# Constants and residual reloads issued by GpSimd, decay loads placed after a batch's three corrections, and a step budget of 1700 in place of 3500

## Chip, cores and metric

The kernel runs on one core of one Trainium2 chip. The metric is the device time of one execution in microseconds (us). Of the kernel before there are three runs: 947.62, 949.55 and 951.24 us, with a median of 949.55 us. The profiled execution, from which all rows below come, took 947.54 us; its span, from the first to the last recorded instruction, is 945.4 us.

## What is computed

Four batches of 768 steps go through three stages. The first is a linear recurrence with complex decays, for 8 heads of 48 channels:

```python
mag = sqrt(a_re**2 + a_im**2); scale = minimum(mag, 0.999) / (mag + 1e-6)
S_re, S_im = ar*S_re - ai*S_im + k v^T, ar*S_im + ai*S_re     # one step t
y[t] = q[t] @ S_re
```

The second is a mixer: with the token weights `u = x + (relu(x^T w_tok1) w_tok2)^T`, then with the channel weights `x2 = u + relu(u w_ch1) w_ch2` (384 to 1536 to 384). The third is a LayerNorm with gain `g_ln` and a second channel layer of the same size: `out = x2 + relu(LN(x2) w_ch1) w_ch2`.

## The kernel before

Rows are put on 128 partitions, three tiles of 128 channels for one batch. Every float32 product that must stay exact is split in two float16 parts, a high and a low one, and is three matmuls (`mm3`, lines 582 to 584).

Four Python generators write the program, and a driver at the end of `tile_kernel` interleaves them.

- `gen_E` does the **decay work** of one batch after the other on VectorE (DVE) and ScalarE (ACT). `gen_A` normalizes the decays and scans them over 16 steps (line 231 on ACT is its first operation; `cmul` is one scan step), `gen_L2` does the second level of the scan on small tiles, and `gen_C` forms the corrections of one tile of 128 channels: cumulated decays, their inverses, and q and k multiplied with them. `gen_C` ends with DMAs (lines 358 and 359) that put q and k into the heads' tiles `stk`. Almost all of its DVE instructions carry line 178, the line of the helper that records them. The decays of a batch lie in one buffer `aj`; `load_a(b, i)` (line 63, SyncE's queue SP) loads tile i of batch b into it, which can start when the corrections of that tile are done with the buffer.
- `gen_P` does the **heads**: 8 for each batch, in TensorE (PE) matmuls of 96 to 128 columns, with copies on ACT and DVE (lines 421 to 500). Their outputs `xh` and `xl` are the x of the mixer.
- `gen_W` splits the weights during the first batch.
- `gen_M` is the **mixing**: for each batch 48 steps, 12 for each half of the tokens and each of the two layers. In a step PE makes 9 matmuls of 384 columns into a bank, `relu_split` (lines 590 and 592) turns it into a high and a low half of `hid` on ACT and DVE, and PE makes 9 more with it. Behind a half's first layer comes `gen_LN`; three steps before the end of its second layer the residual is loaded back into `o` (line 784), which shares its one buffer with the LayerNorm's `xc`. Between two batches stand `tok1` and `tok2`, the token layers: `tok1` reads all eight heads.

What is done beside a mixing step is set by **budgets**. After each step the driver calls `run_E(budget)`, which pulls decay work until its own estimates (the numbers that `gen_E` yields: 470, 870, 1200 and so on) have used the budget up, or until the generator says "wait", which ends the call too. The budget is `EB` in the mixing of batches 2 to 4, `EB0` and `EB1` in that of batch 1, and `ET` in the token layers. All of it stands on line 1127. In the mixing of batch b the decay work is that of batch b+1, and, when that is done, of batch b+2, whose corrections must wait until heads have freed their tiles. The order on each engine follows from this program and from a list scheduler that may move neighbours past each other.

The constants `cst` (identity, mask and others, 129.5 KB) are loaded at line 78 behind the twelve first decay loads in SP's queue; the first operation that needs them is the ACT copy `eye_h` (line 98).

Of the kernel before, what the change touches and what calls it, by code (L numbers as in the profile page):

```python
# [17 lines left out]
B, H, S, D = 4, 8, 768, 48  # L18
# [18 lines left out]
def tile_kernel(ctx: ExitStack, tc: tile.TileContext, a_in, qk_in, v_in, aq2_in, v2_in, wt_in, wm1_in, wm2_in, w64_in, g_in, c_in, out):  # L37
    nc = tc.nc
    V, A, T, G = nc.vector, nc.scalar, nc.tensor, nc.gpsimd
    x2_d = tc.dram_tile([2 * B, 3, P, HB], F32, name="x2_d")  # L40
# [34 lines left out]
    eye_h = ap.tile([P, P], F16, name="eye_h")  # L75
    bias = cp.tile([P, 6], F32, name="bias")
    gl = cp.tile([P, 3], F32, name="gl")
    nc.sync.dma_start(out=cst, in_=c_in)
    wstat = cp.tile([P, 28], F32, name="wstat")
    rstat = cp.tile([P, 6 * B], F32, name="rstat")  # L80
    pstat = cp.tile([P, B, 3 * NCH], F32, name="pstat")
# [109 lines left out]
    def gen_E():  # L191
        V = Rec()
        nxt_q = [load_qk(0, j // 2, j % 2) for j in range(6)]
        load_w(1)
        for b in range(B):
            rec[0] = b == 0
            Ct = ap.tile([P, 3, 6 * 24], F32, tag="I", name="I")
            W = ap.tile([P, 2, 3, NCH], F32, tag="W", name="W")
            sq = ap.tile([P, 2, 3 * NCH], F32, tag="sq", name="sq")
            st = ap.tile([P, 2, 3 * NCH], F32, tag="st", name="st")  # L200
            V.memset(W[:, 0, :, 0:1], 1.0)
            V.memset(W[:, 1, :, 0:1], 0.0)
            for part in PARTS if b == 0 else ((0, 1, 2),):
                for x in gen_A(b, part):
                    yield x
                for x in gen_L2(b, part, Ct, W, sq, st):
                    yield x
                yield "C"
                for i in part:
                    for x in gen_C(b, i, Ct, st, nxt_q):  # L210
                        yield x
                    if b and b + 1 < B:
                        load_a(b + 1, i)
                    yield ("done", b, i)
                if b == 0 and part[-1] == 2:
                    for i in range(3):
                        load_a(1, i)

    av = aj.rearrange("p x (j k r) -> p x j k r", j=6, k=KB)

# [511 lines left out]
    def gen_M():  # L732
# [10 lines left out]
        for b in range(B):  # L743
            for _ in tok2(b, r1, (0, 1, 2) if b else (1, 2)):
                yield "tok"
            ln = iter(())
            if b == 0 and IL < FT:
                g = [mlp(wm1, 0, 0 < LNPE), mlp(wm1, 1, 1 < LNPE, ("sc", "tr", "y"))]
                for s in range(FT + 1 + IL):
                    for half in range(2):  # L750
                        if not 0 <= s - half * IL <= FT:
                            continue
                        k, acc = next(g[half])
                        if half:
                            next(ln, None)
                        if k < FT:
                            yield "step"
                        else:
                            for _ in ln:
                                pass  # L760
                            ln = gen_LN(half, acc)
                            next(ln)
            for half in range(0 if b or IL >= FT else 2, 2):
                for k, acc in mlp(wm1, half, 2 * b + half < LNPE):
                    next(ln, None)
                    if k < FT:
                        yield "step"
                for _ in ln:
                    pass
                ln = gen_LN(2 * b + half, acc)  # L770
                next(ln)
            for half in range(2):
                n = 2 * b + half
                for k, acc in mlp(wm2, half):
                    next(ln, None)
                    if half and b + 1 < B:
                        if k == 2:
                            tokw(b + 1, 0)
                        if k == K_TOK:
                            yield "x"  # L780
                            r1 = tok1(b + 1)
                    if k == FT - 3:
                        o = ap.tile([P, 3, HB], F32, tag="xc", name="o", bufs=1)
                        nc.sync.dma_start(out=o, in_=x2_d[n].rearrange("c p s -> p c s"))
                    if k < FT:
                        yield "step"
                for c in range(3):
                    t = tmp()
                    V.scalar_tensor_tensor(out=t, in0=acc[c][:, 0:HB], scalar=1 / (WS * WS), in1=rs[n], op0=ALU.mult, op1=ALU.mult)
                    V.scalar_tensor_tensor(out=o[:, c], in0=o[:, c], scalar=1 / US, in1=t, op0=ALU.mult, op1=ALU.add)  # L790
                    nc.sync.dma_start(out=out[c, :, n * HB:(n + 1) * HB], in_=o[:, c])
            yield ("done", b)
# [243 lines left out]
    for b in range(B):  # L1036
        k = 0
        while True:
# [21 lines left out]
            for _ in range(2):  # L1060
                n = st["p"]
# [42 lines left out]
NDW = 2  # L1104
CG, CGS = -1, 0
IL = 12
# [17 lines left out]
TGO, TGE, FILL, FK = ("m1", "sc", "m1", "m2"), ("sc", "m2", "m1", "m2"), 0, 0  # L1124
GC, WPE, SPE = 0, 0, 0
YH = 32
SR=1;GC=1;SPE=0;CD=2;LNPE=2;NKICK=0;NKT=1;K_TOK=12;YH=12;NDW=2;NHID=3;NST=3;NV=2;NSK=0;TGO=("m1","sc","m1","m2");PR=0.5;P0=-4;EB=3500;ET=2500;QH=16;WOFF=130;WSTEP=10;EB0=500;EB1=5000;KE=12;DH=1;IL=5;W0=4;NWARM=(0,0);NWB=(0,0);WG=4;WPE=0;EG=7;NWE=0;CGS=0;NS0=6;NSM=99;NSY=3
NV, TH, TP = 3, 4, 3
_INS = ["a", "qk", "v", "aq2", "v2", "wt", "wm1", "wm2", "w64", "g", "c"]

# [55 lines left out]
```

## Time and profile before

| | |
|---|---|
| runs (us) | 947.62, 949.55, 951.24; median 949.55 |
| profiled execution, span (us) | 947.54, 945.4 |
| PE busy | 826.7 us, 87% of the span |
| DVE busy | 736.4 us, 78% |
| ACT busy | 504.5 us, 53% |
| GpSimd (POOL) busy | 59.8 us, 6% |
| chain that ended last | PE 42%, DVE 32%, DMA 10%, issue 7%, ACT 6% |
| DMA | 108.28 MB, mean 115 GB/s |

The page's strip of 40 slices shows three regimes: PE idle and DVE full for the first three slices, both nearly full until about 650 us, and then PE full with DVE at two to six tenths. A busy PE is not yet a PE at its peak, as matmuls overlap; and an engine's idle time counts only where it is on the chain that ends last. The windows below cut the span at `hid` instructions, one stretch for each batch's mixing.

### The profile page before, as it was taken

Reading aid. Unit: us, or ns where it says so; the run is one execution under the profiler, and the core shown is the slowest. Engines: PE = TensorE matmul, PEld = TensorE weight load, DVE = VectorE, ACT = ScalarE, POOL = GpSimd, SP = SyncE. Lnnn points to the kernel's source line nnn. Section 1 sums busy time; section 2 is a strip of 40 time slices with the busy share of each in tenths; the row PEclk is TensorE's granted clock in tenths of the full one; section 3 lists DMA queues with packets and bytes.
Section 4 is the critical chain, followed back from the end, with each engine's and each line's share of the span. In section 5 each row is a group of like instructions: output and inputs, shape, how many; then the busy total and the mean of one; then the engine's idle time right before and its main releaser. Section 6 shows DMA issues by size and latency. Waiting matters only on the chain.

```text
span 945.4 us, 15969 instructions
## 1 busy us (share of the span) xinstructions
PE 826.7 (87%) x5786; PEld 561.7 (59%) x5786; DVE 736.4 (78%) x1588; ACT 504.5 (53%) x1383; POOL 59.8 (6%) x113
## 2 busy tenths in 40 slices
PE   0018998999899899998999998899999999999996
PEld 0007986556567677565666665566766666656563
DVE  6998889999997889987899999897766523264533
ACT  5123356643545586436689952773866524363542
POOL 0000101001030100001100000100000000011110
PEclk9999987999999999998999999899999999999998
DMA  8024576314476350214525010541200102356562
GB/s 291 0 55 119 190 247 209 119 51 169 140 234 179 90 155 14 93 40 127 136 56 148 20 58 33 160 104 60 57 33 26 52 1 92 132 165 215 189 228 95
DMA packets 45287, 108.28 MB, mean 115 GB/s; under 512 B 5904, under 2 KB 28560, under 8 KB 45200
## 3 DMA queue, kind: packets, MB, share of 16 engines
q1 hardware_dynamic: 36816, 61.57, 22.1%
q0 software_dynamic: 8384, 45.62, 14.6%
q8 instruction: 47, 0.77, 0.3%
q14 instruction: 40, 0.33, 0.1%
HBM read 77.20 MB, written 11.01 MB: 93 GB/s over the span
## 4 chain that ended last, share of the span: by engine, by line
PE 42%; DVE 32%; DMA 10%; issue 7%; ACT 6%; SPq 3%; POOL 0%; DVEq 0%; ACTq 0%; POOLq 0%
PE m L583 12%; PE m L582 11%; PE m L584 11%; DVE t L178 6%; DVE aj L178 5%; DVE p L178 4%; DVE hid L592 3%; DMA stk<-t 2%; DMA aj<-in_a 2%; DMA stk<-qk 2%; PE sc L441 2%; DVE pad L533 1%; DMA raw<-in_wm 1%; DVE qk L178 1%; DVE w L549 1%
## 5 line engine op out<-in xcount | busy, mean ns | idle before, releaser
L592 DVE SCALAR_TENSOR_TENSOR hid<-m,hid 128x384 f16<-128x384 f32 x198 | 109.1, 552 | 113.8 <-ACT hid L590 113.3
L582 PE MATMUL m<-u,w 128*128 128x384 f16 x576 | 188.9, 328 | 1.9 <-DVE u L642 1.2
L583 PE MATMUL m<-u,w 128*128 128x384 f16 x576 | 189.0, 328 | 1.3 <-DVE u L703 1.2
L584 PE MATMUL m<-u,w 128*128 128x384 f16 x576 | 188.9, 328 | 0.0
L590 ACT ACTIVATE hid<-m 128x384 f16<-128x384 f32 x198 | 96.0, 485 | 170.8 <-PE m L584 169.7
L583 PE MATMUL m<-hid,w 128*128 128x384 f16 x540 | 176.8, 328 | 8.6 <-DVE hid L592 8.5
L584 PE MATMUL m<-hid,w 128*128 128x384 f16 x540 | 176.7, 328 | 0.0
L584 PEld LDWEIGHTS <-w 128*128 128x128 f16 x1176 | 115.8, 98 | 88.5 <-issue 19.9
L583 PEld LDWEIGHTS <-w 128*128 128x128 f16 x1176 | 116.4, 99 | 73.8 <-issue 4.8
L582 PEld LDWEIGHTS <-w 128*128 128x128 f16 x1176 | 115.6, 99 | 74.0 <-issue 6.3
L582 PE MATMUL m<-hid,w 128*128 128x384 f16 x540 | 127.6, 326 | 1.6 <-ACT hid L590 1.3
L178 DVE SCALAR_TENSOR_TENSOR t<-t 128x384 f32<-128x384 f32 x120 | 64.3, 549 | 8.8 <-ACT t L231 5.7
L428 PE MATMUL m<-cst,stk 96*128 96x96 f32 x10 | 2.5, 377 | 71.1 <-DMA stk<-qk 71.1
L178 DVE TENSOR_TENSOR p<-aj 128x288 f32<-128x288 f32 (+2 forms) x150 | 52.4, 390 | 0.7
L178 DVE TENSOR_TENSOR t<-aj,I 128x768 f32<-128x768 f32 x40 | 36.3, 952 | 12.5 <-DMA stk<-t 9.4
L441 PE MATMUL sc<-stk 96*128 96x128 f32 x300 | 44.8, 284 | 1.2 <-DVE r L446 1.2
L428 PEld LDWEIGHTS m<-cst,stk 96*128 96x128 f32 x10 | 1.8, 231 | 71.4 <-issue 67.5
L441 PEld LDWEIGHTS sc<-stk 96*128 96x128 f32 x300 | 41.0, 197 | 4.1 <-DVE r L446 1.6
L516 POOL DMA_DIRECT2D raw<-in_wm x48 | 25.9, 540 | 213.4 <-DVE sq L561 85.2
L590 ACT ACTIVATION_READ_ACCUMULATOR hid<-m 128x1 f32 x198 | 38.5, 194 | 0.0
L562 ACT ACTIVATE sq<-sq 128x768 f16<-128x768 uint8 x28 | 23.6, 843 | 27.8 <-DVE sq L561 27.8
L536 ACT ACTIVATE w<-raw 128x768 f16<-128x768 f32 x28 | 25.3, 904 | 24.0 <-DVE raw L534 22.7
(273 smaller groups left out, 1692.6 us busy)
## 6 DMA issues: line engine op xcount, KB each, us to landing
raw<-in_wm POOLq DMA_DIRECT2D x48, 768.0 KB, 4.7
qk<-in_qk SPq DMA_DIRECT2D x23, 384.0 KB, 4.5
aj<-in_a SPq DMA_DIRECT2D x9, 768.0 KB, 6.5
stk<-t SPq DMA_DIRECT2D x40, 144.6 KB, 3.3
stk<-qk SPq DMA_DIRECT2D x40, 144.6 KB, 3.1
raw<-in_wt SPq DMA_DIRECT2D x6, 768.0 KB, 5.9
v<-in_v SPq DMA_DIRECT2D x32, 144.0 KB, 2.2
x_d<-xc SPq DMA_DIRECT2D x24, 192.0 KB, 2.2
```

Of the source, the lines that this page charges most:

```text
L178: r = getattr(nc.vector, n)(*a, **k)
L441: last = T.matmul(sc[:, (c % 3) * P:(c % 3 + 1) * P], qc(c, 1), qc(c, 0), start=True, stop=True)
L516: (nc.sync if n < NSY else nc.gpsimd).dma_start(out=raw.bitcast(U8), in_=w_src[n].bitcast(U8)[:, 3:3 + 8 * S])
L533: V.scalar_tensor_tensor(out=pad[0].bitcast(U8).rearrange("p (a b) -> p a b", b=4)[:, :, 3], in0=byte, scalar=3, in1=byte, op0=ALU.logical ...
L536: wact[n] = A.activation(out=dst[:, :, 0], in_=w, func=AF.Copy, scale=WS).ins
L549: wop[n] = V.scalar_tensor_tensor(out=dst[:, :, 1], in0=w, scalar=WS, in1=dst[:, :, 0], op0=ALU.mult, op1=ALU.subtract).ins
L562: A.activation(out=t[:, HB:2 * HB].bitcast(F16), in_=bad_, func=AF.Copy, accum_out=wstat[:, n:n + 1])
L582: T.matmul(out_, wh, xh_, start=first, stop=False)
L583: T.matmul(out_, wh, xl_, start=False, stop=False)
L584: T.matmul(out_, wl, xh_, start=False, stop=last)
L590: A.activation(out=hl[:, 0], in_=p, func=AF.Relu, accum_out=hstat[:, n_h[0]:n_h[0] + 1])
L592: last[:] = [V.scalar_tensor_tensor(out=hl[:, 1], in0=p, scalar=0.0, in1=hl[:, 0], op0=ALU.max, op1=ALU.subtract).ins]
```

## The change

Four edits are made. The constants are loaded from GpSimd's queue in place of SP's. The residual reload `o` goes to GpSimd's queue too. The three decay loads of the next batch are written after the corrections of all three tiles (they stood after each tile for batches 2 and 3; for batch 1 they stood there already). And `EB` is 1700 in place of 3500. In the new file lines above 210 keep their numbers, and those behind are two lower.

```diff
-    nc.sync.dma_start(out=cst, in_=c_in)
+    nc.gpsimd.dma_start(out=cst, in_=c_in)
...
                 for i in part:
                     for x in gen_C(b, i, Ct, st, nxt_q):
                         yield x
-                    if b and b + 1 < B:
+                    yield ("done", b, i)
+                if part[-1] == 2 and b + 1 < B:
+                    for i in range(3):
                         load_a(b + 1, i)
-                    yield ("done", b, i)
-                if b == 0 and part[-1] == 2:
-                    for i in range(3):
-                        load_a(1, i)
...
-                        nc.sync.dma_start(out=o, in_=x2_d[n].rearrange("c p s -> p c s"))
+                        nc.gpsimd.dma_start(out=o, in_=x2_d[n].rearrange("c p s -> p c s"))
...
-SR=1;GC=1;SPE=0;CD=2;LNPE=2;NKICK=0;NKT=1;K_TOK=12;YH=12;NDW=2;NHID=3;NST=3;NV=2;NSK=0;TGO=("m1","sc","m1","m2");PR=0.5;P0=-4;EB=3500;ET=2500;QH=16;WOFF=130;WSTEP=10;EB0=500;EB1=5000;KE=12;DH=1;IL=5;W0=4;NWARM=(0,0);NWB=(0,0);WG=4;WPE=0;EG=7;NWE=0;CGS=0;NS0=6;NSM=99;NSY=3
+SR=1;GC=1;SPE=0;CD=2;LNPE=2;NKICK=0;NKT=1;K_TOK=12;YH=12;NDW=2;NHID=3;NST=3;NV=2;NSK=0;TGO=("m1","sc","m1","m2");PR=0.5;P0=-4;EB=1700;ET=2500;QH=16;WOFF=130;WSTEP=10;EB0=500;EB1=5000;KE=12;DH=1;IL=5;W0=4;NWARM=(0,0);NWB=(0,0);WG=4;WPE=0;EG=7;NWE=0;CGS=0;NS0=6;NSM=99;NSY=3
```

(On the last line only `EB` differs.)

What this does to the order of instructions is shown at three places. First, ACT at the start of the program, before (`t` and `u` are the scratch tiles of the first two decay pieces):

```order
L231 ACTIVATE t<-aj 128x768
L235 ACTIVATE t<-t 128x384
L236 ACTIVATE t<-t,bias 128x384
L237 ACTIVATE t,rstat<-t 128x384
L231 ACTIVATE u<-aj 128x768
L235 ACTIVATE u<-u 128x384
L236 ACTIVATE u<-u,bias 128x384
L98 ACTIVATE eye_h<-cst 128x128
L733 ACTIVATE gstat<-gl 128x3
L541 ACTIVATE eye_w<-cst 128x128
L542 ACTIVATE eye_m<-cst 128x128
L237 ACTIVATE u,rstat<-u 128x384
```

and with the change:

```order
L229 ACTIVATE t<-aj 128x768
L98 ACTIVATE eye_h<-cst 128x128
L539 ACTIVATE eye_w<-cst 128x128
L540 ACTIVATE eye_m<-cst 128x128
L233 ACTIVATE t<-t 128x384
L234 ACTIVATE t<-t,bias 128x384
L235 ACTIVATE t,rstat<-t 128x384
L229 ACTIVATE u<-aj 128x768
L233 ACTIVATE u<-u 128x384
L234 ACTIVATE u<-u,bias 128x384
L731 ACTIVATE gstat<-gl 128x3
L235 ACTIVATE u,rstat<-u 128x384
```

The three copies of the constants moved from behind the second piece's exponent to directly behind the first piece's square; the small operation on the gain `gl` stayed ahead of the second piece's last ACT operation.

Second, DVE where the mixing of batch 2 ends and the token layer of batch 3 begins (the two `hid` rows at the end are those of `tok1`), before:

```order
L178 COPY I<-W 128x36
L178 TENSOR_TENSOR t<-aj,I 128x2x16x24 x4
L789 SCALAR_TENSOR_TENSOR r<-m_6790,rs 128x384
L789 SCALAR_TENSOR_TENSOR r<-m_6791,rs 128x384
L789 SCALAR_TENSOR_TENSOR r<-m_6792,rs 128x384
L178 TENSOR_TENSOR aj<-t 128x2x384 x2
L790 SCALAR_TENSOR_TENSOR o<-o,r 128x384 x2
L592 SCALAR_TENSOR_TENSOR hid<-m_7455,hid 128x384
L790 SCALAR_TENSOR_TENSOR o<-o,r 128x384
L592 SCALAR_TENSOR_TENSOR hid<-m_7456,hid 128x384
```

and with the change:

```order
L178 TENSOR_TENSOR p<-aj 128x288 x2
L178 TENSOR_TENSOR aj<-p 128x6x24 x2
L178 TENSOR_TENSOR p<-aj 128x288 x2
L787 SCALAR_TENSOR_TENSOR r<-m_6444,rs 128x384
L787 SCALAR_TENSOR_TENSOR r<-m_6445,rs 128x384
L787 SCALAR_TENSOR_TENSOR r<-m_6446,rs 128x384
L178 TENSOR_TENSOR aj<-p 128x6x24 x2
L788 SCALAR_TENSOR_TENSOR o<-o,r 128x384 x3
L178 TENSOR_TENSOR p<-aj 128x288 x2
L590 SCALAR_TENSOR_TENSOR hid<-m_7161,hid 128x384
L590 SCALAR_TENSOR_TENSOR hid<-m_7162,hid 128x384
```

Before, the decay work of batch 4 is here through its scan and its second level and in its first correction; with the change it is still in the scan (`p<-aj`, `aj<-p`). Counted over the whole order up to the first of these two `hid` rows, 58 DVE instructions of line 178 stand later with the change: 6 of `p<-aj`, 8 of `aj<-p`, 38 small ones of the second level, 4 of `t<-aj,I` and 2 of `aj<-t`. The program's last line-178 row stands ahead of the 12th `hid` row of the mixing of batch 3 before, and ahead of its 30th with the change. Of the mixings of batch 2 and of batch 3, five `hid` rows follow the last head's last DVE row (`xl`) before, and two with the change.

Third, GpSimd's queue in the second half of the mixing of batch 1 and at the start of the next (`t<-st` and `qk<-st` are the copies that a correction waits for before its DMAs), before:

```order
L516 DMA raw<-in_wm 128x6144
L599 DMA tokw<-tokw_d 128x3072 x2
L332 COPY t<-st 128x3
L332 COPY qk<-st 128x3
L332 COPY t<-st 128x3
L332 COPY qk<-st 128x3
L599 DMA tokw<-tokw_d 128x3072 x2
```

and with the change:

```order
L514 DMA raw<-in_wm 128x6144
L330 COPY t<-st 128x3
L330 COPY qk<-st 128x3
L597 DMA tokw<-tokw_d 128x3072 x2
L782 DMA o<-x_d 128x3x384
L330 COPY t<-st 128x3
L330 COPY qk<-st 128x3
L330 COPY t<-st 128x3
L330 COPY qk<-st 128x3
L782 DMA o<-x_d 128x3x384
L597 DMA tokw<-tokw_d 128x3072 x2
```

The two reloads of batch 1 stand on both sides of the copies of its third correction tile; in SP's queue they are gone.

## Rows read from the trace of the kernel before

**Rows 1.** Windows: length, then PE, PEld, DVE, ACT, POOL busy (instructions), PEclk, DMA.

```profile
179.40:383.90 204.50, 195.02 (x1346) 131.32 (x1345) 190.49 (x371) 111.72 (x291) 19.66 (x27) 1.00 0.41 128
383.90:589.30 205.40, 191.91 (x1460) 125.61 (x1460) 190.24 (x430) 130.81 (x380) 8.90 (x18) 0.98 0.27 76
589.30:651.90 62.60, 57.41 (x440) 38.60 (x440) 53.96 (x91) 40.58 (x111) 5.82 (x9) 0.95 0.45 121
651.90:783.50 131.60, 131.45 (x1022) 87.13 (x1020) 72.83 (x135) 72.39 (x226) 0.00 (x0) 1.00 0.13 39
783.50:934.60 151.10, 149.16 (x932) 90.39 (x933) 66.25 (x133) 71.08 (x200) 13.51 (x25) 1.00 0.51 167
```

**Rows 2.** Windows of line 178 alone, in the mixing of batch 2.

```profile
383.90:589.30 205.40, 107.37 (x255) 0.98 0.27 76
```

**Rows 3.** Waits of PE, 383.9 to 589.3 us: total, times, longest.

```profile
PE m L583 <- DVE hid L592: 6.2, 6, 2.2
PE m L582 <- DVE hid L592: 1.9, 1, 1.9
```

**Rows 4.** Waits of PE, 589.3 to 783.5 us.

```profile
PE m L582 <- DVE hid L592: 3.1, 1, 3.1
PE m L582 <- DVE u L642: 2.4, 4, 0.8
```

**Rows 5.** Timeline of PE around a wait: start, duration, instruction.

```profile
433.94 0.33 PE L584 MATMUL m<-u,w 128*128 128x384 f16 x1
...
439.34 0.52 PE L584 MATMUL m<-hid,w 128*128 128x384 f16 x1
439.66 0.52 PE L583 MATMUL m<-hid,w 128*128 128x384 f16 x1
```

**Rows 6.** Groups of DVE instructions by shape: busy us, mean ns, idle before.

```profile
L178 DVE TENSOR_TENSOR p<-aj 128x288 f32<-128x288 f32 x90 | 36.8, 449 | 0.3
L178 DVE TENSOR_TENSOR t<-aj,I 128x768 f32<-128x768 f32 x40 | 36.3, 952 | 12.5 <-DMA stk<-t 9.4 <-DMA stk<-qk 2.3 <-issue 0.7
L178 DVE TENSOR_TENSOR aj<-p 128x144 f32<-128x144 f32 x90 | 23.3, 299 | 0.3
L178 DVE TENSOR_TENSOR aj<-t 128x768 f32<-128x768 f32 x20 | 18.5, 949 | 0.6 <-DMA aj<-in_a 0.6
```

**Rows 7.** Line 178 by operation: duration in ns, min/median/max.

```profile
L178 DVE TENSOR_TENSOR I<-p x40: 176/243/291, 43.5 to 581.4; 128x126 f32<-128x126 f32 x12, 128x72 f32<-128x72 f32 x8, 128x108 f32<-128x108 f32 x6, 128x84 f32<-128x84 f32 x4
```

**Rows 8.** Timeline of ACT, first 13 us, with the idle time ahead.

```profile
5.75 0.52 ACT L235 ACTIVATE t<-t 128x384 f32<-128x384 f32 x1 [0.62 <-DVE t L178]
...
11.71 0.31 ACT L98 ACTIVATE eye_h<-cst 128x128 f16<-128x128 f32 x1 [1.28 <-DMA cst<-in_c]
11.92 0.19 ACT L733 ACTIVATE gstat<-gl 128x3 f32<-128x3 f32 x1
...
12.42 0.51 ACT L237 ACTIVATE u<-u 128x384 f32<-128x384 f32 x1
```

**Rows 9.** Timeline of DVE, the instruction that this delays.

```profile
13.05 1.15 DVE L178 SCALAR_TENSOR_TENSOR u<-u 128x384 f32<-128x384 f32 x2 [2.09 <-ACT u L237]
```

**Rows 10.** DMA issues: queue, count, KB each, median us to landing.

```profile
raw<-in_wm POOLq DMA_DIRECT2D x48, 768.0 KB, 4.7
...
aj<-in_a SPq DMA_DIRECT2D x9, 768.0 KB, 6.5
...
o<-x_d SPq DMA_DIRECT2D x8, 576.0 KB, 4.1
...
cst<-in_c SPq DMA_DIRECT2D x1, 129.5 KB, 4.4
gl<-in_g SPq DMA_DIRECT2D x1, 1.5 KB, 4.0
```

**Rows 11.** Waits of SP's queue at the residual reload.

```profile
SPq L784 <- DVE u L703: 17.2, 3, 8.4
```

**Rows 12.** Timelines of PE and DVE: a late head's first transposes, its last DVE instruction.

```profile
744.68 0.58 PE L428 MATMUL tr<-cst,stk 96*128 96x96 f32 x5
...
761.89 0.46 DVE L397 SCALAR_TENSOR_TENSOR xl<-y,xh 128x288 f16<-128x288 f32 x1 [1.56 <-ACT xh L396]
```

## Prediction, made before the changed kernel ran

> **What bounds the kernel now.** I read the page's strip first, then windows cut at `hid` rows, then PE's waits in each window, then single rows. The windows [rows 1] have one line for each batch's mixing, and batch 3's is cut in two. In the last two lines PE is busy for 131.45 of 131.60 and 149.16 of 151.10 us: there PE is the bound, and DVE has 72.83 and 66.25 us of work. In the mixing of batch 2 PE is idle for 205.40 - 191.91 = 13.5 us, and in the first 62.6 us of batch 3's for 5.2 us. DVE is busy there for 190.24 us of 205.40 and 53.96 of 62.60. So for these 268 us DVE is about as long as PE, and behind them it is half empty. That is the imbalance on which the change acts.
>
> That PE's idle time comes from DVE is seen in its waits: the longest sums are for `hid` from DVE [rows 3, 4], with one of 3.1 us where `tok2` begins in batch 3. The operations that keep DVE from `hid` are those of line 178, 107.37 us in the mixing of batch 2 [rows 2].
>
> A wait costs more than its length. Before a wait at 434 us a matmul of 384 columns takes 0.33 us and behind it 0.52, and successive ones start 0.32 us apart [rows 5]; the granted clock of the window is 0.98, that of the next 0.95 [rows 1], where the undisturbed ones have 1.00. So a part of each stretch ran at the lower level, 1.2 GHz, after PE had been idle. The loss is 0.02 x 205.4 = 4.1 us in the mixing of batch 2 and 0.05 x 62.6 = 3.1 in the first part of batch 3's.
>
> **Floors.** Idle time and clock loss taken off, PE's own work is 205.4 - 13.5 - 4.1 = 187.8 us in the mixing of batch 2, and 62.6 - 5.2 - 3.1 + 131.5 = 185.8 in that of batch 3. What can be won there is 17.6 and 8.4 us, 26 us in all. Outside these two stretches the change can touch little.
>
> **The step budget.** Up to the first `tok1` row that ends the mixing of batch 2, 58 instructions of line 178 stand later. By their means [rows 6]: 6 x 0.449 + 8 x 0.299 + 4 x 0.952 + 2 x 0.949 = 10.8 us, and 38 small ones at the median of one such group, 0.243 us [rows 7], 9.2; together 20. Rows that follow each other on DVE overlap by nearly 0.1 us, so the engine gets 15 to 20 us back; I take 17. The mixing of batch 2 then has 190.2 - 17 = 173 us of DVE work over a floor of 187.8, 92%; that of batch 3 has 126.8 + 17 = 144 over 185.8, 77%, and instead of ending at the 12th step the decay work ends at the 30th.
>
> What load leaves how much loss is read from the same windows. With DVE work over PE's floor at 190.24/187.8 = 101%, batch 2's mixing loses 17.6 us; at 190.49/195 = 98%, batch 1's loses 9.5; at 53.96/54.3 = 99%, the first part of batch 3's loses 8.3 in 63; at 55% and below 0.2 to 1.9. Between the first two, 3 points of load are worth 8 us in 200. For 92% I take a loss of 5 (bounds 2 and 14), since PE's hand-offs with ACT remain; for 77% spread evenly, 3 (bounds 1.5 and 8.4). Terms: 17.6 - 5 = -12.6 (-15.6 to -3.6), and 8.4 - 3 = -5.4 (-6.9 to 0).
>
> **The constants.** Before, ACT waits at 11.71 us for `cst` with the second piece's last operation behind it, which starts at 12.42 [rows 8]; DVE sits idle for 2.09 us until then [rows 9], and from there on it is full until the first head. With the change the copies stand behind the first square, where ACT has 0.62 us of idle time for some 0.7 us of copies. A load from GpSimd's queue lands after 4.7 us for 768 KB, the constants took 4.4 from SP [rows 10]; issued at about 0.7 us, they land near 5.3, 0.2 us after the square. So this costs about 0.5 us there, and it is absorbed: `gl` is the next that ACT waits for, still ahead of that last operation. By the landing times it was issued at 11.92 - 4.0 = 7.9 us, some 0.6 behind `cst` (11.71 - 4.4 = 7.3); it takes that place now and is read at about 11.3. The operation starts at 11.5, and the head of the program ends 0.9 us sooner. Bounds: -2.0, if `gl` is no limit, and +1.0, if `cst` lands 3 us later than I think. I take -0.9, as the transfer's size is the nearest to a row that I have.
>
> A rule of the Trainium skill speaks against this edit and the next: its page "SBUF — State Buffer", section "A bandwidth-pool intuition that's wrong (but worth ruling out)", says that GpSimd cannot write the descriptors of a DMA while DVE holds the port that they share, and tells of a DMA that went from 620 to 3100 ns. By it the sum would be worse by an estimated 1 to 2 us at the head. The trace does not bear it out: with DVE busy, loads from GpSimd's queue landed in 4.7 us and those of the same size from SP in 6.5 [rows 10].
>
> **The residual reload.** SP's queue waited 17.2 us in three places for LayerNorm to free the buffer [rows 11], with the DMAs of the next corrections behind it. In GpSimd's queue it stands among the copies `t<-st`, which could be held up instead; but the LayerNorm that it waits for is over before the third tile's copies come. The reload is asked for three steps, 9 us, ahead of its use, and lands in 4.1 us from SP and some 5 from GpSimd [rows 10]. SP's gain lies beside DVE work, except in batch 1's mixing; I take -1 (0 to -3).
>
> **The decay loads.** The scheduler puts the first two ahead of the last tile's DMAs, the third at its end, as before for the third. The next decay work begins several steps later than the last correction: in the mixing of batch 2 four `hid` rows, over 11 us, lie between, and a load lands in 6.5 us [rows 10]. Cost 0, covered by those steps; if they went, it is one load's 6.5 us, hidden from PE by DVE's other work or not (0 to +5). Work on PE, ACT and the first batch's heads is the same in number; shifts of order ahead of the mixing I put at 0, within 3 us either way, the size of the shifts in rows 4.
>
> **Sum.** -12.6 - 5.4 - 0.9 - 1 = -19.9. The profiled execution's 947.5 becomes 927.6; it lies 2.0 us below the median of the runs, so I forecast **930 us**, and 919 to 940 for this case alone.
>
> **Rivals.** (1) *The losses are hand-offs, not load.* PE also waits when DVE is early but `hid` must go PE, ACT, DVE, PE, and `hid` from DVE explains 8.1 of the 13.5 us in batch 2's mixing [rows 3]. Then thinner decay work moves them without shortening them: batch 2's mixing keeps 14 of its 17.6 us, batch 3's all, and the head's gain goes into the next wait. 947.5 - 3.6 + 2 = 946 us: no difference. Against it, the second part of batch 3's mixing has all hand-offs with half the DVE load and loses 0.15 us in 131.6 [rows 1]. Chance 0.11.
>
> (2) *The last head comes too late.* With less decay work in a step, corrections end later and the heads crowd at the end of the mixing; `tok1` needs all eight. A head took 761.89 + 0.46 - 744.68 = 17.7 us from its first transposes to its last row among mixing steps [rows 12]. Two `hid` rows, 6 us of PE, follow the last head now, before it was five. If DVE runs three or four steps behind its order there, the mixing's own matmuls run out, PE waits for most of a head, about 13 us, at both batch ends, and each wait is followed by the lower clock for some 2 us: 930 + 2 x 15 = 960 us, slower. For it: in the last nine steps of batch 2's mixing two heads and the next scan meet. Against: DVE has 92% of load there, not over 100. It decides only if the last `xl` falls behind the last `hid` row. Chance 0.07.
>
> (3) *Constants late.* If DVE's work at the start keeps GpSimd from sending its load off, the ACT copies wait, and all of ACT's first operations with them. Without wait and copies the second piece's last operation could start at 12.42 - 1.28 - 0.7 = 10.4 us [rows 8]; with the constants 4 us after the square it starts at 14.4 instead of 11.5, and the time is 933 us. This is what the page named above would lead to. Chance 0.04, since the 4.7 us of GpSimd's loads beside a busy DVE speak against it [rows 10].
>
> **How the numbers follow.** The forecast gets 0.78. Its whole range lies more than 0.5% under the median of before, 949.55 us (0.5% is 4.7 us, about what a measurement of this kernel can tell from no change), and so does rival 3: faster 0.82. Same is rival 1, 0.11, slower rival 2, 0.07. The range takes the forecast's low end, 919, and goes up to 944, between the bounds of the load terms and rival 1; that leaves out about 0.2.
>
> **What would show it right or wrong.** Right: in the mixing of batch 2 a length of about 193 us with PE idle for 3 to 5, DVE busy for some 173, clock 0.99 or 1.00; batch 3's mixing 189; line 178 present until about 690 us; DVE's idle time at 13 us down by 0.9, `eye_h` at 5.3 us; no wait of SP at the reload. Wrong: batch 2's mixing still over 200 us with DVE at 173 (rival 1), a wait of PE over 8 us at `tok1` (rival 2), ACT idle for over 2 us ahead of `eye_h` (rival 3), or a mixing of batch 1 that is longer than its 204.5 us, which I have at no change.

## Result and profile after

The changed kernel takes 940.41 us (median of 4 runs, 938.05 to 943.36) beside 950.39 us for the kernel before on the same chip: a ratio of 0.9892 with a 95% interval of 0.9859 to 0.9926. It is faster by 1.1%, where 2.1% was forecast. The profiled execution took 940.83 us, its span is 939.2 us; against 947.54 of the kernel before that is -6.7 us, where the sum said -19.9.

The windows of the changed kernel, cut at the same `hid` rows (mixings of batches 1 to 4, then the tail), answer to [rows 1]. Columns: length, then PE, PEld, DVE, ACT, POOL busy with their instructions, PEclk, DMA share, GB/s.

```profile
181.00:385.40 204.40, 195.42 (x1343) 131.45 (x1343) 191.87 (x375) 112.38 (x292) 17.55 (x29) 0.99 0.43 127
385.40:581.80 196.40, 187.44 (x1460) 123.81 (x1460) 175.27 (x375) 127.70 (x377) 9.94 (x17) 1.00 0.28 80
581.80:776.90 195.10, 187.99 (x1460) 124.41 (x1459) 142.74 (x282) 114.81 (x341) 13.52 (x16) 0.99 0.23 65
776.90:927.40 150.50, 149.13 (x932) 90.36 (x933) 66.52 (x133) 70.91 (x200) 14.88 (x27) 1.00 0.51 167
```

The mixing of batch 2 is 9.0 us shorter (205.4 to 196.4), with PE idle for 9.0 us in place of 13.5 and the clock at 1.00. The mixing of batch 3, 62.6 + 131.6 = 194.2 us before, is 0.9 us longer. Batches 1 and 4 are within 0.6 us. The stretch from the first PE instruction to the first `hid` of batch 1 took 1.9 us more (113.7 after 111.8), the tail 1.0 more, and the head in front of PE 0.3 less.

Windows of line 178 alone in the mixings of batches 2 and 3; the first is to be read against [rows 2]:

```profile
385.40:581.80 196.40, 90.87 (x199) 1.00 0.28 80
581.80:776.90 195.10, 52.35 (x107) 0.99 0.23 65
```

So 56 instructions and 16.5 us left the mixing of batch 2, as the step budget of the prediction had it (58 and 17).

PE's waits in the mixing of batch 3, which answer to [rows 4]:

```profile
PE m L581 <- DVE hid L590: 3.9, 4, 1.9
PE m L580 <- ACT hid L588: 2.2, 1, 2.2
PE m L580 <- DVE hid L590: 1.1, 1, 1.1
```

The wait of 3.1 us at the start of `tok2` is gone, and two waits of 2 us stand in its place, at 626 and 629 us. Timelines of DVE, then ACT, then PE around them:

```profile
620.20 0.55 DVE L590 SCALAR_TENSOR_TENSOR hid<-m,hid 128x384 f16<-128x384 f32 x1
624.33 1.83 DVE L178 TENSOR_TENSOR t<-aj,I 128x768 f32<-128x768 f32 x2 [3.58 <-issue]
...
628.28 0.55 DVE L590 SCALAR_TENSOR_TENSOR hid<-m,hid 128x384 f16<-128x384 f32 x1
...
624.65 0.44 ACT L419 ACTIVATE dr<-stk 96x288 f32<-96x288 f32 x1 [3.44 <-DMA stk<-qk]
...
626.34 0.65 PE L580 MATMUL m<-hid,w 128*128 128x384 f16 x3 [2.21 <-ACT hid L588]
...
628.88 0.48 PE L581 MATMUL m<-hid,w 128*128 128x384 f16 x1 [1.89 <-DVE hid L590]
```

DVE stands for 3.58 us in front of a correction's `t<-aj,I`, whose scratch tile the DMAs to `stk` still read (other rows of this form name `DMA stk<-t` as the releaser; here the profile names none), and ACT stands for 3.44 us in front of a head's decays on the same DMAs. Then 4 us of other work follow on DVE before its next `hid`, which comes 8.1 us after the last one. PE, which takes one about every 4 us (50 in 195 us), runs dry; and windows ahead of and behind the second wait show what follows:

```profile
625.30:628.70 3.40, 0.65 (x3) 0.29 (x3) 3.40 (x5) 2.86 (x8) 0.75 (x2) 1.00 0.40 118
628.80:632.20 3.40, 3.32 (x11) 1.57 (x11) 3.33 (x7) 1.63 (x3) 0.00 (x0) 0.50 0.00 0
```

After 3.4 us with PE busy for 0.65, PE works for 3.4 us at a granted clock of 0.50, its lower level of 1.2 GHz.

At the head, the timelines of ACT and DVE that answer to [rows 8, 9], with the issue of the gain table `gl` from SP's queue:

```profile
4.89 0.29 ACT L98 ACTIVATE eye_h<-cst 128x128 f16<-128x128 f32 x1
...
7.50 0.34 SPq L89 DMA_DIRECT2D gl<-in_g  x1
...
12.02 0.20 ACT L731 ACTIVATE gstat<-gl 128x3 f32<-128x3 f32 x1 [1.74 <-DMA gl<-in_g]
12.13 0.51 ACT L235 ACTIVATE u<-u 128x384 f32<-128x384 f32 x1
...
12.76 1.15 DVE L178 SCALAR_TENSOR_TENSOR u<-u 128x384 f32<-128x384 f32 x2 [1.95 <-ACT u L235]
```

and the DMA issues that answer to [rows 10]:

```profile
raw<-in_wm POOLq DMA_DIRECT2D x48, 768.0 KB, 4.8
aj<-in_a SPq DMA_DIRECT2D x9, 768.0 KB, 6.4
o<-x_d POOLq DMA_DIRECT2D x8, 576.0 KB, 4.4
cst<-in_c POOLq DMA_DIRECT2D x1, 129.5 KB, 3.4
```

The constants are there when ACT asks for them, without a wait; but ACT now waits 1.74 us for `gl`, and its operation starts at 12.13 us in place of 12.42. At the residual reload SP's 17.2 us of waiting [rows 11] are gone. GpSimd waits in their place, up to 33.6 us for one reload; run 6 below shows that this costs nothing.

### The profile page after: what moved, and what is told of

Its sections match the earlier page's. It is cut to its first block, busy times and chain, and to the rows that moved or that the text cites. A ratio compares the mean times of both kernels' runs of the same rounds, so it can differ in the third digit from the quotient of the medians.

```text
span 939.2 us, 15971 instructions
## 1 busy us (share of the span) xinstructions
PE 825.9 (88%) x5786; PEld 563.3 (60%) x5786; DVE 737.3 (79%) x1588; ACT 503.8 (54%) x1383; POOL 68.3 (7%) x122
## 3 DMA queue, kind: packets, MB, share of 16 engines
q0 software_dynamic: 9584, 50.47, 16.3%
## 4 chain that ended last, share of the span: by engine, by line
PE 33%; DVE 18%; ACT 8%; DMA 2%; issue 2%; SPq 1%; DVEq 0%; ACTq 0%
PE m L580 10%; PE m L581 10%; PE m L582 10%; DVE t L178 5%; DVE aj L178 2%; DVE hid L590 2%; DVE p L178 2%; DMA stk<-t 2%; PE sc L439 1%; ACT hid L588 1%; DVE qk L178 1%; PE tr L466 1%; DMA stk<-qk 1%; ACT hl L447 1%; ACT junk L450 1%
## 5 line engine op out<-in xcount | busy, mean ns | idle before, releaser
L178 DVE TENSOR_TENSOR aj<-p 128x144 f32<-128x144 f32 (+2 forms) x150 | 34.9, 274 | 0.7
```

Source lines behind the costliest of these rows:

```text
L178: r = getattr(nc.vector, n)(*a, **k)
```

## The experiments

Two quantities are used below. **The sum** is DVE's busy time in the mixing of batch 2. **The densest stretch** of a mixing is worked out from a kernel's order of instructions: each instruction of DVE and PE is priced by the trace of the kernel before, and over all pairs of `hid` rows the largest excess of DVE's work over PE's between them is taken. It is an estimate from an order, not a time that a trace shows. Expected times are told by theories: A, the sum of DVE's work in the mixing sets the loss (this is the prediction's load argument); B, C, D, H and S are named where they come.

A ratio comes from several runs; a window comes from one profiled execution. How far a window can be trusted is seen where kernels run the same instructions: the kernel before and runs 1 and 4 differ in `EB` alone, which acts behind the mixing of batch 1, and up to there they took 111.8, 111.1 and 113.5 us for the first heads and 204.5, 205.8 and 206.8 us for the mixing of batch 1. So about 2 us between two windows can be chance. The profiled execution lay 3.8 us above the median of its runs in run 2 and 4.9 above in run 9; it lay 4.2 us below it in run 10 and 3.0 in run 12.

**1. The spread alone.**

```diff
-EB=3500
+EB=1700
```

> The kernel before with one number changed: the due spacing of the decay work (EB) 3500 -> 1700 us-nanoseconds per step; constants, residual reload and decay loads stay as they were. Theory A (spread): all of the gain is here, because it takes DVE work out of mixing 2. Mixing 2 should be 8 to 10 us shorter than the 205.4 us of the kernel before, with DVE busy near 175 us in it, and the ratio to the kernel before 0.988 to 0.991. Mixing 3 should come out near 195 us, no shorter than before, and keep a stall of some 4 us at a step where matmul waits for ScalarE and VectorE behind the scratch reload. Rival B (the queue edits carry it): ratio 0.996 to 1.000, mixing 2 over 202 us.

Measured: 0.9919 (0.9890 to 0.9949), and in the mixings of batches 2 and 3:

```profile
385.50:583.70 198.20, 188.83 (x1460) 124.65 (x1460) 175.61 (x373) 128.62 (x377) 7.27 (x14) 0.99 0.28 79
583.70:779.40 195.70, 188.83 (x1460) 124.63 (x1459) 142.68 (x282) 114.59 (x339) 11.45 (x13) 0.98 0.23 65
```

A little short of what theory A asked, but the place is right: by the medians the spread alone gives three quarters of the gain, and it gives it in the mixing of batch 2.

**2. Everything but the spread.**

```diff
-    nc.sync.dma_start(out=cst, in_=c_in)
+    nc.gpsimd.dma_start(out=cst, in_=c_in)
...
+                if part[-1] == 2 and b + 1 < B:
+                    for i in range(3):
                         load_a(b + 1, i)
...
-                        nc.sync.dma_start(out=o, in_=x2_d[n].rearrange("c p s -> p c s"))
+                        nc.gpsimd.dma_start(out=o, in_=x2_d[n].rearrange("c p s -> p c s"))
```

> The whole change but for the due spacing (EB stays 3500): constants and residual reload in GpSimd's queue, decay loads of batches 2 to 4 when a batch's corrections end. Theory A (spread): ratio 0.998 to 1.001; mixing 2 stays at 203 to 206 us, the head is 0.2 to 0.4 us shorter. Rival B (the queue edits carry it): ratio 0.988 to 0.992. Rival C (the loads in one go cost something that the spread hides): ratio 1.002 to 1.006, mixing 2 or 3 longer by 2 us or more.

Measured: 0.9927 (0.9902 to 0.9952). All theories missed. The window of its mixing of batch 2:

```profile
389.90:587.40 197.50, 189.11 (x1460) 124.73 (x1461) 185.75 (x425) 128.08 (x378) 12.97 (x20) 0.98 0.27 79
```

It is 7.9 us shorter than before with DVE's busy time down by 4.5 only; in the same execution the first heads took 4.3 us more, the mixing of batch 1 2.2 and that of batch 3 2.8. So without the spread the other edits gave nearly as much as the spread alone, which no theory had. Runs 1 and 2 together would give 1.5% by their medians, and the change gives 1.1%; by their intervals it is not shown that the two gains do not add up.

**3. Constants and gain table from GpSimd.**

```diff
-    nc.sync.dma_start(out=cst, in_=c_in)
+    nc.gpsimd.dma_start(out=cst, in_=c_in)
...
-    nc.sync.dma_start(out=gl, in_=g_in)
+    nc.gpsimd.dma_start(out=gl, in_=g_in)
```

> The kernel before with the constants and also the six-number gate table (gl) loaded by GpSimd, so that the table is issued right behind the constants instead of behind SyncE's loads. If the head's limit after the change was that the table lands at 12.0 us, then here ScalarE reads it before 11 us, the first affine on ScalarE runs about 1 us earlier than the 12.42 us of the kernel before, and VectorE's idle time at 13 us shrinks from 2.1 us to about 1 us; ratio 0.998 to 1.000. Rival (a small load takes its 4 us wherever it is issued, and the queue's earlier bytes hold it): table read at 12 us or later, head as in the change, within 0.3 us of before.

Timelines of GpSimd, ACT and DVE at its head:

```profile
2.08 0.54 POOL L89 DMA_DIRECT2D gl<-in_g  x1
...
6.73 0.19 ACT L733 ACTIVATE gstat<-gl 128x3 f32<-128x3 f32 x1
...
11.01 0.52 ACT L237 ACTIVATE u<-u 128x384 f32<-128x384 f32 x1
...
11.66 1.15 DVE L178 SCALAR_TENSOR_TENSOR u<-u 128x384 f32<-128x384 f32 x2 [0.15 <-ACT u L237]
```

The head is as foretold: ACT's operation starts 1.4 us sooner than before and DVE's idle time is 0.15 us. And PE's first instruction comes at 66.2 us in place of 67.6. Yet the time is 1.0015 (0.9989 to 1.0040). The mixing of batch 1 takes 209.1 us, where it took 204.5 to 206.8 with the old order. PE's largest wait there, in this kernel, in the changed kernel, and in run 12, which leaves the constants in SP's queue:

```profile
PE tr L428 <- DMA stk<-qk: 3.9, 1, 3.9
```

```profile
PE tr L426 <- DMA stk<-qk: 3.7, 1, 3.7
```

```profile
PE tr L428 <- DMA stk<-qk: 2.1, 2, 1.4
```

Moving the constants shifts the order of the first heads and of the work behind them, and a head's transposes then wait longer for the DMAs of a correction. That does not explain the longer mixing: the change has nearly the same wait, and its mixing of batch 1 takes 204.4 us. Where the 1.4 us of the head went is open.

**4. The spread at 2300.**

```diff
-EB=3500
+EB=2300
```

> The kernel before with the due spacing (EB) at 2300, between 3500 and 1700. Theory A (VectorE's load in mixing 2 sets its length): VectorE busy in mixing 2 between 175 and 190 us and the length of mixing 2 between 196 and 205 us in the same proportion (0.6 us of length per us of VectorE work taken out), ratio 0.991 to 0.997. Rival D (the gain is an accident of the order, which any other order gives or takes): ratio outside of that, and stage lengths that do not follow VectorE's busy time.

Measured: 1.0043 (1.0020 to 1.0066), slower than before. Theory A falls here. The windows of blocks 85 to 89 (counted in `hid` rows), of the whole mixing of batch 2 and of that of batch 3:

```profile
536.50:561.30 24.80, 23.23 (x222) 17.26 (x221) 24.80 (x56) 23.48 (x72) 0.00 (x0) 1.00 0.10 33
388.00:592.00 204.00, 191.98 (x1460) 125.64 (x1460) 181.28 (x394) 128.98 (x376) 7.51 (x14) 0.98 0.27 77
592.00:791.00 199.00, 188.63 (x1460) 124.73 (x1459) 136.21 (x261) 114.68 (x341) 6.81 (x14) 0.98 0.23 64
```

and of the same blocks 85 to 89 in the kernel before:

```profile
538.40:555.20 16.80, 15.71 (x134) 10.56 (x132) 16.80 (x37) 10.76 (x31) 0.00 (x0) 1.00 0.21 62
```

DVE's sum is 9.0 us below that of before, and the mixing of batch 2 is 1.4 us shorter only. The four blocks take 24.8 us with DVE busy all of it, where the kernel before takes 16.8: heads, the residual and the scan of the next batch meet there, with 25 instructions of line 178 (16 before) among 56 (37 before). But PE is busy too, for 23.23 us of the 24.8, so these blocks are crowded and yet no long wait of PE. And the kernel is not slower than before by its mixing of batch 2: that of batch 3 takes 199.0 us in place of 194.2, with PE idle for 10.4 us in place of 5.3. Why it does is not shown; stage lengths that do not follow DVE's busy time are what rival D (an accident of the order) had foretold.

**5 and 6. The decay loads alone, the residual reload alone.** Each is its hunk of the diff under 2.

> The kernel before with only the decay loads of batches 2 to 4 moved to the end of a batch's corrections. The change without the spread gave 0.9927, with mixing 2 eight us shorter though VectorE's busy time in it fell by only 4.5 us. Theory H (hand-offs: what is lost in mixing 2 are a few places where VectorE or ScalarE stands in front of a scratch tile that a reload of stk still reads, and this edit shifts the corrections so that one of them goes): mixing 2 at 196 to 199 us, VectorE's waits for stk<-t in it down from 7.4 us to 4 or less, ratio 0.991 to 0.995. Rival (the reload of the residual in GpSimd's queue did it): no change, 0.998 to 1.002, mixing 2 at 204 to 206 us.

> The kernel before with only the residual reload in GpSimd's queue. Theory H: ratio 0.998 to 1.001, stages within 1 us of the kernel before. Rival: the reload no longer stands in SyncE's queue ahead of the decay loads and the qk loads, and that alone gives the 8 us of mixing 2: ratio 0.991 to 0.994.

Measured: the loads 0.9954 (0.9937 to 0.9970), the reload 1.0012 (0.9996 to 1.0029). The reload does nothing. The loads give 0.5%, but not where theory H (scratch waits) put it. DVE's waits for the scratch tile in the mixing of batch 2, before and with the loads alone, and the windows of the mixings of batches 2 and 3 with the loads alone:

```profile
DVE t L178 <- DMA stk<-t: 7.4, 3, 3.3
```

```profile
DVE t L178 <- DMA stk<-t: 4.1, 3, 1.8
```

```profile
383.30:589.00 205.70, 190.94 (x1460) 125.16 (x1460) 191.19 (x432) 130.76 (x380) 10.18 (x18) 0.98 0.27 75
589.00:781.40 192.40, 186.32 (x1460) 124.03 (x1459) 126.08 (x224) 111.99 (x337) 5.85 (x9) 1.00 0.24 67
```

The waits for the scratch tile fell from 7.4 to 4.1 us, and the mixing of batch 2 is as long as before. The gain lies in the mixings of batches 1 and 3, 1.4 and 1.8 us. That of batch 1 is more than chance: the three kernels with this order of DVE there (runs 5, 11 and 12) took 203.1, 203.1 and 203.5 us, the three with the old one 204.5 to 206.8.

**7 and 8. Three scratch tiles**, in the kernel before and in the change.

```diff
-NT6, NSTK, NST, NKT, NHID, NR, NTW = 2, 4, 3, 2, 3, 4, 2
+NT6, NSTK, NST, NKT, NHID, NR, NTW = 3, 4, 3, 2, 3, 4, 2
```

> The kernel before with three scratch tiles t in place of two (NT6 2 -> 3), and nothing of the change. The order of the program shifts with it. Theory H: VectorE no longer waits for stk<-t (7.4 us in mixing 2, 2.1 in mixing 3 before; now under 1.5 in each), and mixing 2 loses 4 to 8 us with VectorE's busy time in it at its old 190 us; ratio 0.990 to 0.996. Theory A (VectorE's load in mixing 2 sets it): mixing 2 within 2 us of 205, ratio 0.997 to 1.003.

> The whole change with three scratch tiles. Theory H: the stall of 4 us in mixing 3 (620 to 629 us in the profile of the change) and the two waits of VectorE for stk<-t in mixing 2 (1.5 and 2.1 us) go; ratio to the kernel before 0.980 to 0.986. Theory A: the scratch waits hide under other work of VectorE, ratio 0.988 to 0.991 as the change itself.

Measured: 1.0187 (1.0150 to 1.0224) and 1.0059 (1.0038 to 1.0080), both slower. DVE's waits for the scratch tile in the mixing of batch 2 fell to 4.3 us in run 7 and to 2.0 in run 8, not under 1.5 as foretold for run 7, and that mixing got longer, 208.0 us after 205.4 and 199.5 after the change's 196.4. So theory H falls. The greater loss is in the mixing of batch 1, into which the third tile lets decay work run ahead. Its window in run 7:

```profile
179.10:401.10 222.00, 204.41 (x1341) 136.52 (x1339) 197.45 (x392) 112.67 (x289) 17.06 (x26) 0.95 0.37 115
```

It is 17.5 us longer, with 7 us more of DVE work in it. A wait that bounds how far an engine runs ahead can be worth more than it costs.

**Theory S**, made from these eight runs: what costs time is the densest stretch of DVE's work in each mixing, and not the sum; the supposed reason is that there `hid` is late block after block. It was then used to choose the last four runs.

**9. The change with the spread at 2000**, that is `EB=2000` in place of 1700. **10. The change with idle work**: behind every second `relu_split` of the mixing of batch 2 an instruction on a private tile.

```diff
+        if 50 <= n_h[0] < 98 and n_h[0] % 2 == 0:
+            with tc.issue_after(last[0]):
+                nc.vector.scalar_tensor_tensor(out=zz, in0=zz, scalar=0.0, in1=zz, op0=ALU.add, op1=ALU.add)
```

> The whole change, but the spread set at 2000 in place of 1700. In the order, VectorE gets 178 us of work in mixing 2 (each instruction priced by the trace of the kernel before), more than the 177 us of the run with the spread at 2300 alone, which stayed at 204 us in mixing 2; but the work is not bunched: the largest stretch of steps in which VectorE's work exceeds TensorE's does so by 5.5 us, there by 13.0 us (before: 9.7, the change: 5.3). Theory S (what costs time is the densest stretch of decay work, not the sum over the mixing): mixing 2 at 196 to 200 us, ratio 0.989 to 0.994. Theory A (the sum of VectorE's work in the mixing): mixing 2 at 200 to 205 us, ratio 0.995 to 1.002.

> The whole change, plus 24 idle instructions on VectorE (0.546 us each by the 128x384 rows of the profile, 13 us in all) that nobody waits for, one behind every second hidden block of mixing 2, so that VectorE's work in it is back at 188 us, as in the kernel before, but even. Theory A (the sum): mixing 2 back at 202 to 206 us, ratio 0.996 to 1.002. Theory S (the densest stretch): mixing 2 longer than in the change by 0 to 3 us, ratio 0.988 to 0.994.

Measured: run 9 0.9904 (0.9878 to 0.9930), run 10 0.9933 (0.9911 to 0.9955); both ratios are in the range of S and outside that of A. The lengths that S foretold for the mixing of batch 2 both missed: 203.8 us in run 9 (196 to 200 foretold, and A said 200 to 205) and 191.9 in run 10 (the change's 196.4 and up to 3 more). Windows of the mixings of batches 2 and 3, run 9:

```profile
388.50:592.30 203.80, 192.86 (x1460) 125.51 (x1459) 182.84 (x401) 128.86 (x377) 9.08 (x16) 0.97 0.26 77
592.30:782.10 189.80, 185.76 (x1460) 123.93 (x1461) 135.48 (x258) 113.70 (x341) 9.65 (x16) 1.00 0.24 67
```

and of run 10, with the group of the idle instructions ahead of them:

```profile
L586 DVE SCALAR_TENSOR_TENSOR zz<-zz 128x384 f32<-128x384 f32 x24 | 13.1, 546 | 0.0
```

```profile
385.10:577.00 191.90, 184.60 (x1445) 122.32 (x1445) 178.52 (x380) 128.19 (x377) 9.23 (x16) 1.00 0.28 80
577.00:774.50 197.50, 190.46 (x1477) 125.71 (x1475) 149.26 (x302) 115.21 (x341) 11.32 (x16) 0.99 0.23 66
```

Run 10 is not the test that it was meant to be. The idle instructions were to bring DVE's busy time in the mixing of batch 2 to 188 us; it came to 178.5, as the new order moved other work out of that mixing, some 3 us of PE's too (1445 matmuls in place of 1460). In both mixings together run 10 has 327.8 us of DVE work, 9.8 more than the change's 318.0, and takes 389.4 us to its 391.5. But this is its fastest execution; by the medians run 10 is 0.4% slower than the change, with intervals that overlap. At 0.6 us of length for each us of DVE work, as the expectation of run 4 has theory A, 178.5 us give 0.993, which is what was measured. So run 10 does not tell A from S, and that even work costs less than the same work in a bunch is not shown. Run 9's mixing of batch 2 speaks for theory A, 203.8 us at a clock of 0.97; that of batch 3 is short, 189.8. Its ratio speaks against A: 182.8 us of DVE work would give 0.995 at the same price.

**11. The change without the constants' edit. 12. The kernel before with the decay loads moved and `EB=1500`.**

> The change without the move of the constants: residual reload, decay loads and spread alone. Moving the constants shifts work in the first heads and made mixing 1 denser (densest stretch 12.3 us over TensorE against 10.5 before), which took back more than the 0.3 us of the head. Densest stretches here 10.5, 2.9 and 3.4 us (sum 16.8; the change 20.7, before 28.0). Theory S: ratio 0.984 to 0.989, two to five us below the change. Theory A (VectorE's sum in mixing 2 as in the spread alone, 175 us): 0.989 to 0.993.

> The decay loads as in the change and the spread at 1500, nothing else. Densest stretches 10.5, 2.1 and 3.1 us (sum 15.7, the smallest of the orders looked at). Theory S: the fastest version, ratio 0.983 to 0.988, mixing 2 at 193 to 196 us. Theory A: as the spread alone, 0.989 to 0.993. Theory D (accident of the order): anywhere from 0.985 to 1.000.

Measured: 0.9866 (0.9837 to 0.9894) and 0.9859 (0.9833 to 0.9885), both in the range of S and the two fastest, with medians of 937.13 and 935.19 us beside 949.26. Theory A's ranges were told for 175 us of DVE work in the mixing of batch 2; the profiles have 167.8 and 172.5. With these, at 0.6 us for each us, A gives 0.986 and 0.989: run 11 fits it as well as S, and run 12 lies just outside. Run 12's windows, mixings of batches 1 to 3:

```profile
178.40:381.90 203.50, 194.60 (x1346) 131.26 (x1345) 189.84 (x371) 112.74 (x291) 19.98 (x27) 1.00 0.42 129
381.90:574.30 192.40, 187.02 (x1460) 124.13 (x1460) 172.52 (x368) 127.78 (x377) 7.06 (x14) 1.00 0.29 83
574.30:769.20 194.90, 187.95 (x1460) 124.32 (x1459) 144.57 (x289) 114.38 (x341) 11.59 (x14) 0.99 0.23 63
```

Its mixing of batch 2 takes 192.4 us with PE idle for 5.4, about what the prediction had asked of the change (193 us and 3 to 5) and a little under what S foretold (193 to 196). Run 12 beats the kernel before by 1.4%. Its interval overlaps that of the change, so that it beats the change too is likely, not shown.

All kernels, by the sum of their densest stretches (mixings of batches 1, 2, 3, in us), with DVE's busy time and the length of the mixing of batch 2:

| kernel | densest stretches | sum of them | DVE, mixing 2 | length, mixing 2 | ratio |
|---|---|---|---|---|---|
| 12 loads, EB 1500 | 10.5, 2.1, 3.1 | 15.7 | 172.5 | 192.4 | 0.9859 |
| 11 change without constants | 10.5, 2.9, 3.4 | 16.8 | 167.8 | 190.8 | 0.9866 |
| 1 spread alone | 10.5, 5.2, 3.1 | 18.8 | 175.6 | 198.2 | 0.9919 |
| 10 change and idle work | 12.3, 4.4, 3.4 | 20.1 | 178.5 | 191.9 | 0.9933 |
| **the change** | 12.3, 5.3, 3.1 | 20.7 | 175.3 | 196.4 | 0.9892 |
| 9 change, EB 2000 | 12.3, 5.5, 3.2 | 21.0 | 182.8 | 203.8 | 0.9904 |
| 2 all but the spread | 12.3, 5.7, 5.9 | 23.9 | 185.8 | 197.5 | 0.9927 |
| 5 loads alone | 10.5, 9.8, 5.6 | 25.9 | 191.2 | 205.7 | 0.9954 |
| 3 constants and gl | 12.3, 9.7, 4.8 | 26.8 | 190.4 | 205.4 | 1.0015 |
| **before** | 10.5, 9.7, 7.8 | 28.0 | 190.2 | 205.4 | 1 |
| 6 reload alone | 10.5, 9.7, 7.8 | 28.0 | 190.2 | 205.6 | 1.0012 |
| 4 spread 2300 alone | 10.5, 13.0, 5.7 | 29.2 | 181.3 | 204.0 | 1.0043 |
| 8 change, three tiles | 16.3, 12.0, 9.0 | 37.3 | 177.8 | 199.5 | 1.0059 |
| 7 three tiles alone | 24.3, 6.3, 8.3 | 38.9 | 188.7 | 208.0 | 1.0187 |

(The lengths of runs 10 and 11 are some 3 us too short for a comparison, since that much of PE's work moved to the mixing of batch 3.)

Over these 14 kernels the ratio goes with the sum of the densest stretches (correlation 0.95) and less with DVE's busy time in the mixing of batch 2 (0.58; without runs 7 and 8 it is 0.94 and 0.75). DVE's busy time in the mixings of batches 1 and 2 added up reaches 0.76. Stage by stage the picture is another. The length of the mixing of batch 2 by itself goes better with DVE's busy time in it (0.86) than with its own densest stretch (0.69), and that of batch 3 hardly goes with its densest stretch at all (0.14). Runs 4 and 9 have nearly equal loads in the mixing of batch 2 and densest stretches of 13.0 and 5.5, and take 204.0 and 203.8 us. So S is a rule for the whole time, found by looking at ten of the fourteen kernels and then right for the ratios of the other four; that dense stretches are the cause is not shown. Rival D, that a new order gives or takes time by accident, is not excluded for any single kernel; against it stand the four ratios. None of the runs keeps the order and changes the load alone, as the scheduler rearranges the whole order for each edit. One thing more stands in the profiles: in the mixing of batch 2 PE's granted clock is 1.00 in the change and in runs 8, 10, 11 and 12, and lower in the nine other kernels; the four shortest are among those five.

## Why the prediction was right or wrong

Its forecast's mechanism held in part (faster, through thinner decay work in the mixing of batch 2, as run 1 shows), at about half the size, 940.41 us where it said 930 and a range of 919 to 944. What it did not see is run 2: the edits to which it gave 1.9 us reach 0.9927 without the spread, and their gain lies for the most part in that same mixing. Their parts alone, runs 5 and 6, gave 0.5% and nothing; the constants alone were not run, so this stays open. By its steps:

- **Step budget, the work moved.** Right. DVE is busy for 175.3 us in the mixing of batch 2 (said: 173) and 142.7 in that of batch 3 (144); the last row of line 178 starts at 693 us (690).
- **Batch 2's mixing, -12.6.** It measured -9.0 with the rest of the change and -7.2 with the spread alone (run 1). The step that was mis-sized is "For 92% I take a loss of 5": the load was 93% of the floor, and the loss 196.4 - 187.8 = 8.6. It lay within the bounds of 2 and 14. Loss was read as a function of load, from a few windows of one kernel, and load alone does not set it: run 2 loses 9.7 us at 99% of the floor, runs 4 and 9 lose 16.2 and 16.0 at 97%. What does is open; the densest stretch of this mixing does not tell run 4 (13.0) from run 9 (5.5).
- **Batch 3's mixing, -5.4.** It measured +0.9, outside the bounds (-6.9 to 0). The step that failed is "for 77% spread evenly, 3": the work is not even. It comes as corrections, each with its DMAs and a scratch tile to wait for, and the rows at 620 to 632 us show one such place with two waits of PE and 3.4 us of the lower clock. Rival 1 had this mixing keep all its loss, and it did, in runs 1 and 12 too (195.7 and 194.9 us), though at this place by waits for DMAs. For the mixing of batch 2 rival 1 is refuted by the change and by runs 1 and 12, in which PE's idle time fell from 13.5 us to 9.0, 9.4 and 5.4.
- **The constants, -0.9.** The head came 0.3 us sooner. `cst` was in time (`eye_h` at 4.89 us; said 5.3). The step that failed is that `gl` "takes that place now and is read at about 11.3": issued at 7.50 us, it was read at 12.02, after 4.5 us and not 4.0. Run 3 shows that this was the limit, and that the 1.4 us that can be had there do not show in the whole time (1.0015). Rival 3 did not come: ACT does not wait ahead of `eye_h`. Nor did the rule that the prediction cites from the Trainium skill ("SBUF — State Buffer", "A bandwidth-pool intuition that's wrong (but worth ruling out)") show itself in these loads: `cst` landed in 3.4 us from GpSimd after 4.4 from SP, and with DVE busy GpSimd's loads of 768 KB landed in 4.8 us. The page tells its case of a DVE `tensor_copy`; only 10 of DVE's 1588 instructions are copies, so the rule itself is not tested here.
- **The residual reload, -1.** It is worth nothing (run 6: 1.0012). So SP's 17.2 us of waiting cost nothing either.
- **The decay loads, 0 (0 to +5).** Alone they gain 0.5% (run 5). My bounds left out a gain without a reason. The loads' place changes the order of the work behind them, and with the new order the mixing of batch 1 is shorter in runs 5, 11 and 12; that the order is the reason is likely, not shown.
- **Rival 2, the last head too late.** Not in the change: no wait of PE at `tok1` above 1.5 us. At a budget of 2300 (run 4) heads and the next scan do meet in the last blocks, but PE is busy for 23.2 of those 24.8 us, so the long wait that rival 2 describes did not come there either. Its price for the lower clock, some 2 us behind a wait, is short: behind the two waits shown above it lasted 3.4 us.
- **Outside the sum** I had 0 within 3 us. The first heads took 1.9 us more, the tail 1.0 more, and the mixings of batches 1 and 4 0.7 less together. With -9.0, +0.9 and the 0.3 us at the head this makes the 6.2 us between the two spans. The 1.9 us can be chance: with one and the same order the first heads took 110.7 us in run 12 and 114.7 in run 11.

## What to carry to other kernels

An engine's busy share over a stage says that it may be the limit, not what relief is worth. Adding up both engines' work between the points where one waits for the other, and looking for the densest stretch, went with the time of fourteen versions of this kernel, and the version with the lowest median was found by it. It is a guide for choosing what to try, not an explanation: for the mixings of batches 2 and 3 by themselves the load told more. Where a scheduler rebuilds the whole order, an edit's own effect (1.4 us at the head in run 3) can fail to show in the whole time, so edits are to be timed one by one and together, and not judged by the place that they aim at. A buffer that holds an engine back can be what keeps its work even: a third one made the kernel 1.9% slower. And a window of one execution is weak evidence for a difference of 2 us.

## What the runs showed of the hardware

- A load's size hardly set its time at the start of the program: the 1.5 KB of `gl` took 4.0 and 4.5 us from SP and, in run 3, 3.8 from GpSimd; the 129.5 KB of `cst` took 4.4 from SP and 3.4 and 4.3 from GpSimd. What counts for such a small table is where in the queue it is issued: at 7.50 us from SP's, read at 12.02; at 2.08 us from GpSimd's (run 3), there when ACT asked at 6.73.
- PE's granted clock went to 0.50 for 3.4 us after the two waits at 626 and 629 us, 4 us of waiting in all. So a place with two short waits cost more than its idle time.
